# Attention on one Trainium2 core: exponentials of the first and third step transposed by the tensor engine instead of by DMA

## The chip, the cores and the metric

The kernel runs as one program on one core of a Trainium2 chip. The core has a tensor engine (PE, whose weight loads the profile lists as PEld), a vector engine (DVE), a scalar engine (ACT), GpSimd (POOL) and a sync engine (SP); 16 DMA engines move data for it. The metric is the device time of one execution in microseconds (us). Three executions of the kernel before took 1034.42, 1036.01 and 1037.72 us.

## What is computed

Three layers follow each other: causal attention with a cumulative bias, a mixture of eight experts with a greedy assignment of tokens, and a feed-forward layer. The change lies in the first one:

```python
# q, k, v: (4, 8, 576, 64), s: (4, 8, 576)
scores = scale * q @ k.T
cum = np.cumsum(np.maximum(s, 0.0), axis=-1)
bias = -(cum[:, :, :, None] - cum[:, :, None, :])
scores = np.where(causal, -1e9, scores + np.minimum(bias, 0.0))
attn = np.exp(scores - scores.max(-1, keepdims=True))
attn = attn / (attn.sum(-1, keepdims=True) + 1e-9)
out = attn @ v            # then x = out as (2304, 512)
# expert layer: logits = x @ w_gate; tokens taken in the order of all logits,
# 288 to an expert; relu(x[mask] @ w1[e]) @ w2[e]
# last layer: h = x @ w_in; (max(h,0) + alpha*min(h,0)) @ w_out
```

## The kernel before

The 32 heads are worked off as 16 pairs p, and each pair in four steps i: step 0 takes query blocks 0 and 1 of 128 rows (both heads), step 1 block 2, step 2 block 3, step 3 the last 64 queries of both heads. All operands are split into a high and a low half, and a product is made of three matmuls (high by high, low by high, high by low).

One step passes through these functions. `qk` (lines 166 to 191, PE) makes the scores in a PSUM tile `sc`, of which there are two, and adds the causal mask (line 181) and the bias (lines 182 and 191). The bias is a matmul of two small operands, SB and MB, which `load_bias` (lines 98 to 106) loads by DMA for two pairs at a time (`hb`, two pairs). `mins` (198, 199, DVE) takes the row minimum, `exps` (205, 208, ACT) writes the exponentials `e` in fp32, 128 queries by keys. For the product with v the keys must lie on the partitions. So `split_hi` (217, 221, 222, DVE) rounds e to fp16 in `eh`, `split_lo` (228, 231, 232, POOL) writes the remainder beside it, and `etr` (235, SP's queue) transposes both by one DMA from SBUF to SBUF into `et`. Four steps later (LAG=4) `av` (250 to 252 and 256 to 260, PE) multiplies et by v. `norm_main` (275, DVE), `finish` (286), and the logits of the router (`lg_T`, 294, four fp32 transposes by PE into a tile `tp`; `lg_act`, 298; `lg_pe`, 304; `lg_dve`, 309 and 310) close the pair. Of the PSUM tiles `tp` there are three.

Every engine works its instructions off in program order. That order is written by hand as a list of events: each function gets a time in steps, and a place within the step from the tuple ORDER, with a correction per function from the table SH:

```python
def at(t,eng,f,*a):
    u=t+ORDER.index(eng)/16+SH.get(key(f,a),0)
    ev.append((u,f,a))
```

From step 51 on, weights of the last layer are loaded early, and from step 54 on 11 of them are converted beside attention: three DVE instructions each (607 to 609), a copy on ACT (580) and a subtraction on POOL (581). After attention, `Router.phase` (line 489 on) and the expert and feed-forward layers run; their buffers are taken from pools that are opened when the pool `ap` of attention is closed, in the same memory (lines 947 to 950).

Of the kernel before, what the change touches and what calls it, by code (L numbers as in the profile page):

```python
# [28 lines left out]
LAG=4  # L29
LQ=(-12,-8)  # L30
LV=(-10,-9,-6,-5,-4)
LB=-7
V0=(1,1,1)
TI=-2
TQ=0;TD=1;TE='act2'
# [2 lines left out]
TP1=0  # L38

SH={"lg_pe": 1.83, "lt_act": 0.1, "v2_pool": 0.06, "spin": 0.17, "finish_tail": -0.2, "rd_4": 2.79, "lg_dve": 1.56, "load_bias": 0.68, "lt_pe": 1.31, "v3_act1": -0.94, "rd_2": -0.13, "v3_act0": 0.03, "etr2": 0.79, "rd_3": 1.2, "finish": 0.07, "lt_dve": 0.94, "av1": 1.9, "lt_T": -0.2, "av2": 0.43, "etr0": 0.23, "norm_main": 0.37, "v3_dve0": 1.63, "v3_dve1": 0.11, "av0": 1.59, "etr3": 0.23, "split_lo0": 0.07, "split_lo1": 0.6, "split_hi2": -0.23, "split_lo2": -0.13, "split_hi3": 0.63, "split_lo3": 0.77}  # L40
ORDER=('pe0','pe1','pe2','pe3','dve0','dveA','dveB','act1','sp','dve2','act2','dve3','pl','act3','ld')
def attention(tc, q, k, v, s, w_gate, xd, L, C, cp, ap, psum, dp, hook=None, rawp=None):
    rawp=rawp or ap
    nc=tc.nc
# [18 lines left out]
    nc.sync.dma_start(st, s.rearrange("b h s -> (b h) s"))  # L63
    for nm in 'qk': load_qk1(0,nm,0)

    SB=[ap.tile([128,2304],R,name=f'sb{i}') for i in range(2)]
    MB=[ap.tile([128,2,576],R,name=f'mb{i}') for i in range(2)]
    nc.vector.memset(SB[0].bitcast(F),0.0)
    mk=ap.tile([128,128],BF,name='mk'); nc.gpsimd.memset(mk,0.0)
    nc.gpsimd.affine_select(out=mk,in_=mk,pattern=[[-1,128]],compare_op=OP.is_ge,fill=1e9,base=0,channel_multiplier=1)  # L70
# [18 lines left out]
    def init_bias(i):  # L89
        sf=SB[i].bitcast(F); mf=MB[i].bitcast(F)  # L90
        nc.gpsimd.memset(mf,0.0)
        nc.gpsimd.memset(mf[64:66],1.0)
        if i: nc.vector.memset(sf,0.0)
        for h in range(4):
            r=32*(h%2)
            for c0,n in ((512*h,512),(2048+64*h,64)):
                nc.gpsimd.memset(sf[r:r+2,c0:c0+n],-1.0)
    def load_bias(hb):
        i=hb%2
        hv=chd[4*hb:4*hb+4]  # L100
        mf=MB[i].bitcast(F)
        mv=hv.rearrange("(p h) t s -> h t p s",h=2)
        for h in range(2): nc.sync.dma_start(mf[32*h:32*h+2], mv[h])
# [60 lines left out]
    PARTS={0:((0,0),(1,128)),1:((2,0),),2:((3,0),)}  # L164
    WID={0:384,1:384,2:512}
    def qk(p,i):
        hb=p//2; sb,mb=SB[hb%2],MB[hb%2][:,p%2]
        kh,kl=OPS['k',p]; qh,ql=OPS['q',p]
        sc=SM[p,i]=psum.tile([128,2,512],F,name='sc',bufs=2)
        if i<3:  # L170

            for ti,off in PARTS[i]:
                N=128*(ti+1)
                qs=slice(128*ti,128*ti+128)
                for n,(x,y) in enumerate(((qh,kh),(ql,kh),(qh,kl))):
                    for h in range(2):
                        r=slice(64*h,64*h+64)
                        nc.tensor.matmul(sc[:,h,off:off+N],x[r,qs],y[r,:N],start=(n==0),stop=False)  # L178
                for h in range(2):
                    c0=512*(2*(p%2)+h)+128*ti  # L180
                    nc.tensor.matmul(sc[:,h,off+N-128:off+N],idb,mk,start=False,stop=False,skip_group_check=True)
                    nc.tensor.matmul(sc[:,h,off:off+N],sb[:,c0:c0+128],mb[:,:N],start=False,stop=True)  # L182
        else:
            for h in range(2):
                o=sc[:,h,:288]
                ks=slice(288*h,288*h+288)
                nc.tensor.matmul(o,qh[:,512:640],kh[:,ks],start=True,stop=False)
# [723 lines left out]
def body(tc, q, k, v, s, w_gate, w1, w2, w_in, w_out, alpha, cfd, cbd, cid, out):  # L911
    nc = tc.nc
    with ExitStack() as c:
        cp = c.enter_context(tc.tile_pool(name="cp", bufs=1))
        dp = c.enter_context(tc.tile_pool(name="dp", bufs=1, space=bass.MemoryType.DRAM))
        c.enter_context(tc.manual_schedule())
        c.enter_context(nc.allow_low_precision(reason="integers and split operands"))
        cf = cp.tile([128, NCF], F, name="cf")
        ci = cp.tile([128, NCI], I, name="ci")
        cb = cp.tile([128, 256], BF, name="cb")  # L920
        nc.sync.dma_start(cf, cfd)
        L = cp.tile([128, 18, 8], F, name="L")
# [83 lines left out]
```

## Time and profile before

| | |
|---|---|
| median of three runs | 1036.01 us |
| the profiled execution | 1033.37 us, of which its span is 1031.6 us |
| busy in the span | PE 919.2, PEld 848.6, DVE 634.0, POOL 527.7, ACT 440.4 us |
| first row minimum of pair 0 (line 198) | starts at 15.83 us |
| last logits added (line 310) | start at 274.55 us |
| mean granted TensorE clock | 0.917 |

The views of the trace give times in us from the start of the span. PE's busy time counts each matmul to its modelled end, so a short gap can vanish in it. "Clock" is the share of full speed that TensorE was granted; in this trace it is 1.00 or 0.50 in nearly every stretch of 2 us, that is 2.4 or 1.2 GHz.

### The profile page before, as it was taken

How to read it: one execution, taken by the hardware profiler on the slowest of the kernel's cores; microseconds unless marked ns; L12 is line 12 of the kernel's file. 1: busy time of each engine (PE TensorE's matmuls, PEld its weight loads, DVE VectorE, ACT ScalarE, POOL GpSimd, SP SyncE). 2: the span in 40 equal slices, each digit the busy share in tenths (PEclk: the TensorE clock that was granted, in tenths of full speed). 3: DMA queues.
4: the chain of work that ended last, by engine and by line, in shares of the span. 5: the costliest groups of instructions: out<-in, count | busy, mean ns of one | idle time of the engine just before them, and what ended most of it. 6: DMA issues, size and time to landing. Idle time of an engine off the chain costs nothing.

```text
span 1031.6 us, 20621 instructions
## 1 busy us (share of the span) xinstructions
PE 919.2 (89%) x7883; PEld 848.6 (82%) x7883; DVE 634.0 (61%) x1238; ACT 440.4 (43%) x1106; POOL 527.7 (51%) x457
## 2 busy tenths in 40 slices
PE   6889998986427899899999999999999999999995
PEld 4667776765416789899999999999999899999994
DVE  6867667779894987776675645744654642442310
ACT  4656666544212334433334334334434344444432
POOL 6756766755423646744355346526625434634422
PEclk9968879867557999999999999999999999999997
DMA  5998999897577102222343315307304422522200
GB/s 167 206 215 170 213 193 204 198 265 141 146 265 233 40 20 79 81 65 87 63 111 104 51 46 147 73 8 162 89 9 90 123 52 61 152 53 65 52 1 24
DMA packets 219891, 116.59 MB, mean 113 GB/s; under 512 B 148304, under 2 KB 202960, under 8 KB 219792
## 3 DMA queue, kind: packets, MB, share of 16 engines
q1 hardware_dynamic: 180144, 96.78, 38.8%
q10 hardware_dynamic: 36576, 9.05, 5.8%
q0 software_dynamic: 3072, 9.44, 3.1%
q8 instruction: 62, 1.02, 0.4%
q14 instruction: 37, 0.30, 0.1%
HBM read 70.92 MB, written 9.58 MB: 78 GB/s over the span
## 4 chain that ended last, share of the span: by engine, by line
PE 55%; DVE 16%; DMA 10%; issue 8%; POOL 6%; ACT 3%; SPq 0%; POOLq 0%; DVEq 0%; ACTq 0%
PE hp L655 8%; PE hp L656 7%; PE hp L657 7%; PE acc L685 7%; PE acc L687 7%; PE acc L686 7%; DMA et<-eh 4%; DMA out_dram<-stg,idt 3%; PE sc L178 3%; PE sc L182 2%; PE mi L460 2%; DVE g L667 1%; DVE mn L198 1%; DVE eh L217 1%; DVE a L609 1%
## 5 line engine op out<-in xcount | busy, mean ns | idle before, releaser
L673 POOL TENSOR_TENSOR hh<-g,hh 128x288 fp32r<-128x288 f32 x128 | 118.4, 925 | 243.4 <-ACT hh L672 213.8
L667 DVE SCALAR_TENSOR_TENSOR g<-g,nal 128x288 f32<-128x288 f32 x128 | 79.6, 622 | 160.0 <-ACT g L666 153.3
L228 POOL TENSOR_TENSOR eh<-e,eh 128x768 f16<-128x768 f32 (+1 forms) x48 | 97.0, 2023 | 61.3 <-DVE eh L217 45.5
L581 POOL TENSOR_TENSOR w0r<-wraw,w0r 128x512 fp32r<-128x512 f32 x62 | 89.0, 1436 | 58.4 <-ACT w0r L580 58.2
L665 ACT ACTIVATE g<-hp 128x288 f32<-128x288 f32 x128 | 52.2, 408 | 131.5 <-PE hp L657 117.1
L672 ACT ACTIVATE hh<-g 128x288 fp32r<-128x288 f32 x128 | 56.9, 444 | 120.0 <-DVE g L667 117.9
L685 PE MATMUL acc<-hh,rB 128*128 128x288 f32 x352 | 106.1, 301 | 0.0
L687 PE MATMUL acc<-hh,rB 128*128 128x288 f32 x352 | 104.2, 296 | 0.0
L686 PE MATMUL acc<-hh,rB 128*128 128x288 f32 x352 | 104.0, 296 | 0.0
L205 ACT ACTIVATE e<-sc,mn 128x128 f32<-128x128 f32 (+3 forms) x128 | 66.0, 524 | 77.6 <-DVE mn L198 40.1
L655 PE MATMUL hp<-x2h,rB 128*128 128x288 f32 x320 | 90.8, 305 | 0.0
L656 PE MATMUL hp<-x2h,rB 128*128 128x288 f32 x320 | 89.7, 300 | 0.5 <-POOL rB L581 0.5
L661 DVE SCALAR_TENSOR_TENSOR hh<-hp,hh 128x288 fp32r<-128x288 f32 x64 | 29.0, 454 | 84.4 <-ACT hh L660 84.4
L686 PE MATMUL acc<-hh,w1r 128*128 128x288 f32 x256 | 76.7, 300 | 1.7 <-DVE w1r L581 0.8
L685 PE MATMUL acc<-hh,w1r 128*128 128x288 f32 x256 | 77.0, 301 | 0.0
L687 PE MATMUL acc<-hh,w1r 128*128 128x288 f32 x256 | 76.1, 297 | 0.0
L655 PE MATMUL hp<-xTh,w0r 128*128 128x288 f32 x256 | 73.7, 308 | 0.9 <-ACT xTh L708 0.6
L656 PE MATMUL hp<-xTh,w0r 128*128 128x288 f32 x256 | 73.0, 304 | 0.4 <-POOL w0r L581 0.4
L198 DVE TENSOR_REDUCE mn<-sc 128x2 f32<-128x256 f32 (+1 forms) x64 | 50.5, 810 | 33.5 <-PE sc L182 33.5
L685 PEld LDWEIGHTS acc<-hh,rB 128*128 128x128 f32 x352 | 66.4, 189 | 0.3
L687 PEld LDWEIGHTS acc<-hh,rB 128*128 128x128 f32 x352 | 66.5, 189 | 0.0
L581 POOL TENSOR_TENSOR w1r<-wraw,w1r 128x512 fp32r<-128x512 f32 x46 | 63.9, 1389 | 4.8 <-ACT w1r L580 4.6
(252 smaller groups left out, 2918.2 us busy)
## 6 DMA issues: line engine op xcount, KB each, us to landing
wraw<-in_moe_w_dram SPq DMA_DIRECT2D x128, 256.0 KB
rB<-in_moe_w_out_dram SPq DMA_DIRECT2D x11, 512.0 KB
qr<-in_q_dram SPq DMA_DIRECT2D x16, 320.0 KB
vr<-in_v_dram SPq DMA_DIRECT2D x40, 128.0 KB
rB<-in_moe_w_in_dram SPq DMA_DIRECT2D x10, 512.0 KB
kr<-in_k_dram SPq DMA_DIRECT2D x16, 288.0 KB
xd<-xm SPq DMA_DIRECT2D x16, 256.0 KB
rA<-in_moe_w_in_dram SPq DMA_DIRECT2D x4, 512.0 KB
```

The source lines that it names most:

```text
L198: nc.vector.tensor_reduce(mn[:,2*z:2*z+2],sc[:,:,off:off+128*(ti+1)],axis=AX.X,op=OP.min)
L205: nc.scalar.activation(e[:,h,off:off+N],sc[:,h,off:off+N],AF.Exp,bias=mn[:,2*z+h:2*z+h+1],scale=-1.0,accum_out=den[:,2*ti+h:2*ti+h+1])
L228: nc.gpsimd.tensor_sub(e4[:,:,1],e[:,:,:N],e4[:,:,0])
L581: lo_eng.tensor_sub(l,x,h.bitcast(F))
L655: nc.tensor.matmul(ps,wh[k],x[0][:,k],start=(k==0),stop=False)
L656: nc.tensor.matmul(ps,wl[k],x[0][:,k],start=False,stop=False)
L657: for k in range(4): nc.tensor.matmul(ps,wh[k],x[1][:,k],start=False,stop=(k==3))
L667: nc.vector.scalar_tensor_tensor(g,g2[:,1],self.nal[:,f:f+1],g,op0=OP.mult,op1=OP.add)
L673: nc.gpsimd.tensor_sub(hh[:,1],g,hh[:,0].bitcast(F))
L685: nc.tensor.matmul(a,wh[:,ds],hh[:,0],start=(f==0),stop=False)
L686: nc.tensor.matmul(a,wl[:,ds],hh[:,0],start=False,stop=False)
L687: nc.tensor.matmul(a,wh[:,ds],hh[:,1],start=False,stop=(f==last))
```

## The change

Steps 0 and 2 of every pair (PEI) no longer use split_hi, split_lo and the DMA. Instead, for each of the two heads, `etT` transposes e in fp32 blocks of 128 by 128 by PE into a tile tp (three blocks in step 0, four in step 2), `etA` (ACT) copies tp as fp16 into the high half of et, and `etL` (DVE) subtracts that from tp and writes the low half. Steps 1 and 3 keep the old way. The table ETS gives the places: for head 0, PE's place pe0 of the next step (before the scores), act2 and dve3; for head 1, pe3 and act3 of the next step, and dve1 of the one after it. ORDER gets the new place dve1, so the places behind it move by a sixteenth of a step.

The operands of the bias are held and loaded per pair, at half the size, 4 instead of 7 steps ahead (LB). The router's pool `rp` is opened before attention, with memory of its own.

```diff
-LB=-7
+LB=-4
...
-ORDER=('pe0','pe1','pe2','pe3','dve0','dveA',...,'act3','ld')
+ORDER=('pe0','pe1','pe2','pe3','dve0','dve1','dveA',...,'act3','ld')
+PEI=(0,2)
+ETS=(((1,'pe0'),(1,'act2'),(1,'dve3')),((1,'pe3'),(1,'act3'),(2,'dve1')))
...
-    SB=[ap.tile([128,2304],R,name=f'sb{i}') for i in range(2)]
-    MB=[ap.tile([128,2,576],R,name=f'mb{i}') for i in range(2)]
+    SB=[ap.tile([128,1152],R,name=f'sb{i}') for i in range(2)]
+    MB=[ap.tile([128,576],R,name=f'mb{i}') for i in range(2)]
...
-    def load_bias(hb):
+    def load_bias(p):
+        i=p%2
+        hv=chd[2*p:2*p+2]
+        for h in range(2): nc.sync.dma_start(MB[i].bitcast(F)[32*h:32*h+2], hv[h])
...
+    def etT(p,i,h):
+        if h==0: SM['T',p,i]=ap.tile([128,WID[i]//32,128],H,name=f'et{i}',bufs=2)
+        e=SM['e',p,i]
+        if h: SM.pop(('e',p,i)); SM.pop(('mn',p,i))
+        tp=SM['tp',p,i,h]=psum.tile([128,512],F,name='tp',bufs=TPB)
+        for j in range(WID[i]//128): nc.tensor.transpose(tp[:,128*j:128*j+128],e[:,h,128*j:128*j+128],idf)
+    def et2(p,i,h):
+        e4=SM['T',p,i].rearrange("p (h t j) q -> p h t (j q)",h=2,t=2)
+        return e4[:,h,0],e4[:,h,1],SM['tp',p,i,h][:,0:WID[i]]
+    def etA(p,i,h):
+        hi,lo,tp=et2(p,i,h)
+        nc.scalar.activation(hi,tp,AF.Copy)
+    def etL(p,i,h):
+        hi,lo,tp=et2(p,i,h); SM.pop(('tp',p,i,h))
+        nc.vector.tensor_sub(lo,tp,hi)
...
+    for p in range(1,NP): at(4*p+LB,'ld',load_bias,p)
...
-        at(t+1,'sp',split_hi,p,i); at(t+1,'sp',split_lo,p,i)
-        at(t+1+TD,TE,etr,p,i)
+        if i in PEI:
+            for h in range(2):
+                for (d,e),f in zip(ETS[h],(etT,etA,etL)): at(t+d,e,f,p,i,h)
+        else:
+            at(t+1,'sp',split_hi,p,i); at(t+1,'sp',split_lo,p,i)
+            at(t+1+TD,TE,etr,p,i)
...
+        rp = c.enter_context(tc.tile_pool(name="rp", bufs=1))
         with ExitStack() as a:
             ap = a.enter_context(tc.tile_pool(name="ap", bufs=1))
...
-            rp = a.enter_context(tc.tile_pool(name="rp", bufs=1))
```

PE, around the scores of a step 2 (`sc<-kh,qh 128x512`), before:

```order
L294 MATMUL tp<-cf,xm 128x128 x4
L178 MATMUL sc<-kh,qh 128x512 x2
L178 MATMUL sc<-kh,ql 128x512 x2
L178 MATMUL sc<-kl,qh 128x512 x2
L181 LDWEIGHTS idb
L181 MATMUL sc<-mk,idb 128x128
L182 MATMUL sc<-mb_92,sb_90 128x512
```

and now (L310 is the old L294, L243 is etT on the exponentials of step 0):

```order
L310 MATMUL tp<-cf,xm 128x128 x4
L243 MATMUL tp<-cf,e 128x128 x3
L178 MATMUL sc<-kh,qh 128x512 x2
L178 MATMUL sc<-kh,ql 128x512 x2
L178 MATMUL sc<-kl,qh 128x512 x2
L181 LDWEIGHTS idb
L181 MATMUL sc<-mk,idb 128x128
L182 MATMUL sc<-mb_95,sb_93 128x512
L181 LDWEIGHTS idb
L181 MATMUL sc<-mk,idb 128x128
L182 MATMUL sc<-mb_95,sb_93 128x512
L243 MATMUL tp<-cf,e 128x128 x3
```

Three transposes of head 0 now stand between the logits' transposes and the scores of step 2, and those of head 1 behind these scores, ahead of the next `av`; the eight of step 2 stand in the same way around the scores of the next pair's step 0.

DVE, from the row minimum of a step 1 (`L198 ... x1` ahead of L144 or L310) to the fp16 rounding of that step, before:

```order
L198 TENSOR_REDUCE mn<-sc 128x2
L144 TENSOR_SCALAR vh_e<-tp 128x1
L217 CAST eh<-e 128x2x384
L129 SCALAR_TENSOR_TENSOR ql<-qr,qh 128x640
L267 RECIPROCAL rd<-rd 128x9
L198 TENSOR_REDUCE mn<-sc 128x2
L217 CAST eh<-e 128x2x384
```

and now (L252 is etL; L326 is the old L310, L283 the old L267):

```order
L198 TENSOR_REDUCE mn<-sc 128x2
L326 TENSOR_TENSOR L<-L,tp 128x32
L144 TENSOR_SCALAR vh_e<-tp 128x1
L129 SCALAR_TENSOR_TENSOR ql<-qr,qh 128x640
L252 TENSOR_TENSOR et_2063<-tp,et_2063 128x384
L283 RECIPROCAL rd<-rd 128x9
L198 TENSOR_REDUCE mn<-sc 128x2
L252 TENSOR_TENSOR et_2063<-tp,et_2063 128x384
L217 CAST eh<-e 128x2x384
```

The first of the two CASTs is gone, and a subtraction from PSUM stands on either side of the row minimum of step 2.

SP, from one output of a pair (`xd<-xm`) to the next, before:

```order
L286 DMA xd<-xm 128x4x128
L235 DMA_TRANSPOSE et_1262<-eh 128x16x128
L289 DMA xd<-xtl 256x1x64 x2
L235 DMA_TRANSPOSE et_1300<-eh 128x9x128
L57 DMA kr<-in_k_dram 128x576
L235 DMA_TRANSPOSE et_1348<-eh 128x12x128
L61 DMA vr<-in_v_dram 128x256
L235 DMA_TRANSPOSE et_1417<-eh 128x12x128
```

and now:

```order
L302 DMA xd<-xm 128x4x128
L103 DMA mb_94<-chd 2x576 x2
L105 DMA sb_92<-chd 2x2x512
L106 DMA sb_92<-chd 2x2x64
L305 DMA xd<-xtl 256x1x64 x2
L235 DMA_TRANSPOSE et_1406<-eh 128x9x128
L60 DMA kr<-in_k_dram 128x576
L64 DMA vr<-in_v_dram 128x256
L235 DMA_TRANSPOSE et_1530<-eh 128x12x128
```

Two transposes of a pair are left of four, and the four small loads of the next pair's bias stand behind the output, now for every pair.

## Rows read from the trace of the kernel before

**Rows 1.** Stretches (us; busy, instructions; clock, DMA share, GB/s): pairs 0-12, 13-15, rest.
```profile
15.83:198.76 182.93, 163.47 (x1683) 128.84 (x1683) 130.53 (x220) 112.94 (x323) 121.34 (x90) 0.85 0.99 203
198.76:274.55 75.79, 55.34 (x516) 45.24 (x514) 68.81 (x97) 33.51 (x90) 46.28 (x32) 0.70 0.81 181
274.55:1031.60 757.05, 692.58 (x5637) 668.32 (x5637) 425.15 (x912) 290.59 (x688) 348.70 (x306) 0.95 0.33 85
```

**Rows 2.** Waits, 15.83 to 198.76 us: total, times, longest.
```profile
PE av L250 <- DMA et<-eh: 12.2, 7, 3.6
```

**Rows 3.** Stretches, same columns (PE PEld DVE ACT POOL): an idle PE, then ten us.
```profile
176.00:179.00 3.00, 0.00 (x0) 0.00 (x0) 1.49 (x3) 1.92 (x6) 1.55 (x1) 1.00 0.95 161
181.00:191.00 10.00, 10.00 (x58) 8.01 (x54) 4.37 (x10) 3.30 (x13) 4.16 (x4) 0.50 1.03 236
```

**Rows 4.** Stretches of one pair each, same columns: pairs 2, 7, 9 and 10.
```profile
39.80:51.73 11.93, 10.32 (x133) 8.02 (x131) 9.29 (x18) 8.85 (x25) 9.13 (x9) 1.00 1.09 206
113.33:126.00 12.67, 10.80 (x139) 8.60 (x137) 10.95 (x18) 8.56 (x25) 9.04 (x7) 1.00 1.11 220
140.70:155.95 15.25, 15.14 (x141) 11.96 (x140) 11.09 (x18) 8.82 (x26) 8.77 (x6) 0.69 1.03 192
155.95:168.68 12.73, 12.05 (x150) 9.85 (x148) 9.15 (x18) 8.74 (x25) 8.77 (x9) 1.00 1.04 205
```

**Rows 5.** DMA queues: packets, MB, share of 16 engines; q10 is ACT's.
```profile
q10 hardware_dynamic: 36576, 9.05, 5.8%
```

**Rows 6.** PE in order of time: start, us; at full and at half clock.
```profile
129.33 0.60 PE L294 MATMUL tp<-cf,xm 128*128 128x128 f32 x4
129.86 0.50 PE L178 MATMUL sc<-kh,qh 64*128 64x512 f32 x2
...
146.36 1.05 PE L294 MATMUL tp<-cf,xm 128*128 128x128 f32 x4
147.21 0.64 PE L314 MATMUL tp<-cf,xtl 128*128 128x128 f32 x2
```

**Rows 7.** Groups by shape, 0 to 262 us, and line 709: busy us, mean ns.
```profile
L217 DVE CAST eh<-e 128x768 f16<-128x768 f32 x32 | 21.6, 675 | 13.8 <-DMA et<-eh 11.6 <-ACT e L205 1.6 <-POOL kl L130 0.6
L217 DVE CAST eh<-e 128x1024 f16<-128x1024 f32 x16 | 18.3, 1143 | 5.2 <-DMA et<-eh 3.9 <-ACT e L205 0.8 <-issue 0.5
L228 POOL TENSOR_TENSOR eh<-e,eh 128x768 f16<-128x768 f32 x32 | 62.5, 1952 | 46.0 <-DVE eh L217 45.5 <-PE sc L182 0.5
L228 POOL TENSOR_TENSOR eh<-e,eh 128x1024 f16<-128x1024 f32 x16 | 34.7, 2166 | 15.3 <-DVE rd L269 15.3
L298 ACT ACTIVATE xT<-tp 128x512 f32<-128x512 f32 x15 | 8.9, 593 | 0.0
L709 DVE TENSOR_TENSOR xTl<-mi,xTh x6: 545/558/558, 315.5 to 421.7; 128x384 fp32r<-128x384 f32 x6
```

**Rows 8.** Lines 608 and 609, early conversions: ns minimum/median/maximum, first and last start.
```profile
L608 DVE SCALAR_TENSOR_TENSOR a<-rA,a x7: 691/1642/2019, 211.7 to 258.0; 128x512 int32<-128x512 int32 x7
L609 DVE SCALAR_TENSOR_TENSOR a<-rA,a x7: 1529/2009/2106, 215.6 to 259.7; 128x512 int32<-128x512 int32 x7
```

**Rows 9.** DVE and PE near the start, in order of time.
```profile
9.49 1.98 DVE L93 MEMSET sb<- 128x2304 f32 x1 [0.43 <-issue]
...
12.14 0.47 PE L178 MATMUL sc<-kl,qh 64*128 64x128 f32 x2 [2.55 <-DVE kl L130]
```

**Rows 10.** DVE from attention to the router, in order of time.
```profile
274.68 1.18 DVE L811 TENSOR_SCALAR nal<-al 128x16 f32<-128x16 f32 x1
...
275.86 0.30 DVE L496 TENSOR_REDUCE m<-L 128x18 f32<-128x144 f32 x1
```

**Rows 11.** Chain of waits near the start: start, us, what.
```profile
10.95 1.98 DMA sb<-chd
```

**Rows 12.** SP's queue and PE, from an output to the next pair's first bias.
```profile
127.92 0.38 SPq L286 DMA_DIRECT2D xd<-xm  x1
...
137.93 0.46 PE L182 MATMUL sc<-mb,sb 128*128 128x128 f32 x1
```

More of the change, by code (lines that the diff above doesn't have):

```diff
@@ L40 @@
 SH={"lg_pe": 1.83, "lt_act": 0.1, "v2_pool": 0.06, "spin": 0.17, "finish_tail": -0.2, "rd_4": 2.79, "lg_dve": 1.56, "load_bias": 0.68, "lt_pe": 1.31, "v3_act1": -0.94, "rd_2": -0.13, "v3_act0": 0.03, "etr2": 0.79, "rd_3": 1.2, "finish": 0.07, "lt_dve": 0.94, "av1": 1.9, "lt_T": -0.2, "av2": 0.43, "etr0": 0.23, "norm_main": 0.37, "v3_dve0": 1.63, "v3_dve1": 0.11, "av0": 1.59, "etr3": 0.23, "split_lo0": 0.07, "split_lo1": 0.6, "split_hi2": -0.23, "split_lo2": -0.13, "split_hi3": 0.63, "split_lo3": 0.77}
-ORDER=('pe0','pe1','pe2','pe3','dve0','dveA','dveB','act1','sp','dve2','act2','dve3','pl','act3','ld')
+ORDER=('pe0','pe1','pe2','pe3','dve0','dve1','dveA','dveB','act1','sp','dve2','act2','dve3','pl','act3','ld')
+PEI=(0,2)
+ETS=(((1,'pe0'),(1,'act2'),(1,'dve3')),((1,'pe3'),(1,'act3'),(2,'dve1')))
 def attention(tc, q, k, v, s, w_gate, xd, L, C, cp, ap, psum, dp, hook=None, rawp=None):
@@ L93, in init_bias @@
         if i: nc.vector.memset(sf,0.0)
[L94 to L97, printed above, removed]
-    def load_bias(hb):
[L99 to L103, printed above, removed]
+        for h in range(2):
+            for c0,n in ((512*h,512),(1024+64*h,64)):
+                nc.gpsimd.memset(sf[32*h:32*h+2,c0:c0+n],-1.0)
+    def load_bias(p):
+        i=p%2
+        hv=chd[2*p:2*p+2]
+        for h in range(2): nc.sync.dma_start(MB[i].bitcast(F)[32*h:32*h+2], hv[h])
         sv=hv.rearrange("h t s -> t h s")
-        nc.sync.dma_start(SB[i].bitcast(F)[64:66,0:2048].rearrange("t (h s) -> t h s",h=4), sv[:,:,0:512])
-        nc.sync.dma_start(SB[i].bitcast(F)[64:66,2048:2304].rearrange("t (h s) -> t h s",h=4), sv[:,:,512:576])
+        nc.sync.dma_start(SB[i].bitcast(F)[64:66,0:1024].rearrange("t (h s) -> t h s",h=2), sv[:,:,0:512])
+        nc.sync.dma_start(SB[i].bitcast(F)[64:66,1024:1152].rearrange("t (h s) -> t h s",h=2), sv[:,:,512:576])
     init_bias(0)
@@ L166, in qk @@
     def qk(p,i):
-        hb=p//2; sb,mb=SB[hb%2],MB[hb%2][:,p%2]
+        hb=p//2; sb,mb=SB[p%2],MB[p%2]
         kh,kl=OPS['k',p]; qh,ql=OPS['q',p]
@@ L179, in qk @@
                 for h in range(2):
-                    c0=512*(2*(p%2)+h)+128*ti
+                    c0=512*h+128*ti
                     nc.tensor.matmul(sc[:,h,off+N-128:off+N],idb,mk,start=False,stop=False,skip_group_check=True)
@@ L190, in qk @@
                 if h: nc.tensor.matmul(sc[:,h,224:288],idb,mkt,start=False,stop=False,skip_group_check=True)
-                nc.tensor.matmul(o,sb[:,2048+128*(p%2):2048+128*(p%2)+128],mb[:,ks],start=False,stop=True)
+                nc.tensor.matmul(o,sb[:,1024:1152],mb[:,ks],start=False,stop=True)
     def mins(p,i):
@@ L359, in attention @@
         for z in range(5): at(8*hb+LV[z],'ld',load_v1,hb,z)
-        at(8*hb+LB,'ld',load_bias,hb)
         v_events(hb,8*hb-1)
@@ L368, in attention @@
             if i<3 or h==1: at(t,'act1',exps,p,i,h)
-        at(t+1,'sp',split_hi,p,i); at(t+1,'sp',split_lo,p,i)
-        at(t+1+TD,TE,etr,p,i)
+        if i in PEI:
+            for h in range(2):
+                for (d,e),f in zip(ETS[h],(etT,etA,etL)): at(t+d,e,f,p,i,h)
+        else:
+            at(t+1,'sp',split_hi,p,i); at(t+1,'sp',split_lo,p,i)
+            at(t+1+TD,TE,etr,p,i)
         at(t+LAG,'pe2',av,p,i)
```

## The prediction

> **What bounds the kernel now.** I read the stretches first, cut at the row minima that begin the pairs. The stage after attention lasts 757 us [rows 1], and none of its instructions is changed. In the first 13 pairs (182.9 us, 14.07 us a pair) no engine is busy all the time: PE 163.5, DVE 130.5, POOL 121.3, ACT 112.9 us; but the 16 DMA engines have a share of 0.99 [rows 1]. So DMA sets the mean pace. How it does so is seen in the waits and then in short stretches. PE waits 12.2 us in 7 waits for a transposed tile et, at most 3.6 us [rows 2]; this is the direct loss. Behind such a gap comes a second one: from 176 to 179 us PE does nothing, and from 181 to 191 it runs at half clock (0.50, so 1.2 GHz), busy all the 10 us, with DVE, ACT and POOL under half busy [rows 3]. The mean clock of the 13 pairs is 0.85 [rows 1]; with two levels, that is 30% of the time at 1.2 GHz, 55 us. Pairs in which the clock stays at 1.00 last 11.93, 12.67 and 12.73 us, and PE is busy for 10.32, 10.80 and 12.05 us of them; pair 9, at 0.69, lasts 15.25 with PE busy for 15.14 [rows 4]. PE's work of a pair is thus about 11.06 us at full clock (the mean of the three). In pair 9 the low share is 9.5 us, so 5.75 us at full clock did 0.52 of the work and the 9.5 us the other 0.48: 19.8 us a pair at half clock.
>
> The last three pairs (75.8 us) are another stage: with the early conversions DVE is busy for 68.8 us [rows 1], and PE, at a mean of 0.70, for 55.3. DVE bounds them.
>
> **The change, part by part.**
>
> *DMA, SP, POOL.* A pair's transposes carry 1536, 1536, 2048 and 1152 columns of 128 fp16; the first and third go, 0.92 of 1.61 MB. The only DMA kind that I can price alone is the 39 transposes of ACT's queue, 9.05 MB in 5.8% of the span, 6.6 us of all 16 engines for 1 MB [rows 5]. By that 6.1 us a pair go, and DMA needs 13.9 - 6.1 = 7.9 us a pair. The per-pair bias adds 32 small issues for 32 transposes less. POOL loses one subtraction of 1.95 and one of 2.17 us a pair [rows 7], 4.1 of 9.3. What is left on both is hidden under PE.
>
> *PE.* It gains 6 + 8 = 14 fp32 transposes of 128x128 a pair. The same operation on xm takes from 129.33 to 129.86 for four at full clock, 0.133 us each, and 0.213 at half clock (146.36 to 147.21) [rows 6]. So 1.86 us a pair: 11.06 becomes 12.9 us at full clock, 19.8 becomes 22.8 at half.
>
> *ACT.* Two copies of 512 columns at 0.593 [rows 7] and two of 384, below that, are at most 2.4 us on top of 112.9/13 = 8.7: 11.1 us, under PE.
>
> *DVE.* A pair loses a CAST of 0.675 and one of 1.143, and gains two subtractions from PSUM of 384 columns (0.558 for the same shape in line 709) and two of 512 [rows 7]. No row has the latter; scaled by columns 0.74, with the 0.558 and twice it as ends. Sum +2.60 - 1.82 = +0.8 a pair: 10.0 becomes 10.8, again under PE's 12.9.
>
> *Pace of pairs 0 to 12.* What is late next when the transposed tiles are not? PE itself, the highest sum. An engine with work queued does not idle long, so I expect the clock to stay near 1.00. From 12.9 as lower end and 14.07 (nothing gained) as the other I take 13.2, near the lower end, because the full-clock pair with most work idles only 0.7 us beside its 12.05 [rows 4]. 13 x 13.2 = 171.6 against 182.9: **-11.3 us**.
>
> *Pairs 13 to 15.* DVE's 68.8 us grow by 3 x 0.8 = 2.4. Against that its early conversions run long beside POOL: line 608 takes 0.69 at the least but 1.64 at the median, line 609 has a median of 2.01 [rows 8]. Taking 0.69 as the free time for both, the 14 instructions of these two groups lose about 7 x 0.95 + 7 x 1.32 = 16 us. POOL works 46.3 us in this stage and loses 3 x 4.1 = 12.3 of them, 27%; if the loss shrinks alike, 4.3 us come back (ends: 0 and 16). DVE idles 7.0 us of the stage; a transpose waited for is half as likely, so I keep 3.0. 68.8 + 2.4 - 4.3 + 3.0 = 69.9 against 75.8: **-5.9 us**.
>
> *Start.* The clearing of SB, 1.98 us for 2304 columns, stands ahead of kl on DVE, for which PE then waits 2.55 us [rows 9]. At half the size 1.0 us goes: **-1.0 us**.
>
> *Edits at nothing.* The router's first reduction starts at 275.86, when DVE is done with line 811, which began behind the last logits [rows 10]; a buffer of its own starts no earlier. If that cover were gone it could be worth the 1.2 us of line 811 and no more. The bias load: a pair's four loads stand behind an output such as that at 127.92, and the next pair's first bias matmul comes at 137.93 [rows 12]. The first such load took 1.98 us [rows 11]. Even with the pair 1.5 us shorter it is there in time.
>
> The sum is -18.2 us. The profiled execution took 1033.4 us, 2.6 under the median of 1036.0, so I expect 1015.2 in an execution like it and **1017.8 us** in the median.
>
> **Rivals.**
>
> *The clock keeps falling (ends slower).* All PE waits need not come from DMA. If the low clock keeps its 30% of the time, a pair takes 1/(0.30/22.8 + 0.70/12.9) = 14.8 us, the 13 pairs gain 9.9 us, and with -6.9 from the rest the time is 1039. The point that decides is a pace of 14.6, a low share of about 0.28; at half of the old share (13.8 us) it would be 1025. For it: more PE work makes each slow stretch dearer. Against it: the slow stretch that I looked at follows a PE that does nothing at all [rows 3], while DMA was full. The Trainium skill, page "TensorE: Matmul & The Clock Gate", section "Part 4: PE-mode transpose", says that transposes don't count as work for the clock gate as matmuls do. By that rule the added 1.86 us a pair would not help to hold the clock, and this rival would be the forecast; no row here shows a long run of transposes, and the four at 129.33 ran at full clock among matmuls. Chance 0.13.
>
> *DVE's queue becomes the bound.* Each of the four subtractions of a pair waits for its copy on ACT, which stands behind exponentials, and two row minima of later steps stand behind a subtraction. With DVE at 10.8 us of work, a pace of 14.6 is reached when each of these waits is 0.95 us long; at 1.2 us the pace is 15.6, 13 pairs gain 19.9, and with the last three giving nothing it is 1055. For it: a copy of 0.59 and a handover make a part of such a wait plain. Against: DVE has 2.4 us free in 13.2. Chance 0.07.
>
> *The transposes that are left come late all the same.* If half of the bytes cost nearly as much DMA time as all, PE goes on waiting for step 1 and step 3 and nothing changes but the added work hides in the waits: 1035. Against: a share of 0.99 has to fall when bytes go. Chance 0.05.
>
> *More than forecast.* The busy time of PE counts modelled ends, so its real need may be 12.4; with DVE's contention gone by half (-8) and its idle time by 6: 13 x 12.4 gives -21.7, in all 1036 - 21.7 + 2.4 - 8 - 6 - 1 = 1002. Chance 0.10.
>
> **How the numbers follow.** Forecast 0.65, clock 0.13, DVE 0.07, no effect 0.05, more 0.10. The forecast's own bounds (pace 12.9 to 14.07, the last pairs from 0 to -12) reach from 1007 to 1035. With the bounds and the rivals near them, 1001 to 1038 holds about 8 in 10. 0.3%, 3.1 us, is about what a measurement of this kernel can tell from no change. Faster: 0.65 and 0.10, with a third of the clock's rival: 0.79. Within: the no-effect case and a third of the clock's: 0.09. Slower: the rest, 0.12.
>
> **What would show it.** In the changed profile: a DMA share near 0.6 to pair 12; a clock above 0.95 there; pairs near 13.2 us with PE busy for some 13; few waits of PE for et; POOL near 5.3 us a pair; lines 608 and 609 shorter. A clock still at 0.85, DVE idle in front of the new subtractions for more than 0.95 us each, or waits for et of the old size would prove the rivals. A share of DMA still near 1 would break the whole argument, and so would a stage after attention that is not 757 us long.

## The result, and the profile after

The changed kernel takes 1049.62 us (median of four runs, 1047.29 to 1050.30); the kernel before took 1035.40 beside it (1034.42 to 1037.72). The ratio is 1.013 with a 95% interval of 1.0106 to 1.0154. The forecast was 1017.8 us in a range up to 1038: it missed, on the slow side.

The parts that were forecast for DMA and POOL did happen. The page's busy times after, and the queue that carries the transposes:

```profile
PE 938.2 (89%) x8107; PEld 865.8 (83%) x8107; DVE 626.9 (60%) x1270; ACT 470.1 (45%) x1170; POOL 449.9 (43%) x417
...
q1 hardware_dynamic: 121840, 82.10, 30.0%
```

POOL works 450 us instead of 528. The same three stretches as in [rows 1] (pairs 0 to 12, pairs 13 to 15, the rest; columns as there):

```profile
14.30:212.24 197.94, 175.15 (x1851) 139.19 (x1852) 133.80 (x245) 135.02 (x373) 63.35 (x64) 0.91 0.58 131
212.24:290.17 77.93, 59.73 (x573) 48.74 (x570) 63.42 (x103) 39.77 (x104) 30.03 (x25) 0.75 0.51 131
290.17:1048.50 758.33, 695.56 (x5637) 671.70 (x5637) 422.03 (x912) 291.89 (x689) 349.59 (x306) 0.95 0.33 84
```

DMA's share falls from 0.99 to 0.58, and yet the first 13 pairs take 15.0 us longer. The profiled span grew by 16.9 us: the start gives 1.5 back, pairs 0 to 12 cost 15.0, pairs 13 to 15 cost 2.1, and the rest 1.3. So the cause lies in the pairs. PE's waits there, total, times, longest (before, [rows 2], it was et from DMA):

```profile
PE tp L320 <- DVE et L252: 7.1, 5, 1.4
PE tp L243 <- DVE L L325: 4.8, 3, 1.6
PE tp L243 <- ACT e L205: 4.4, 8, 1.3
PE tp L330 <- DVE L L326: 3.2, 2, 1.6
```

No wait for et is left in these pairs. PE now waits to write a tile `tp`. L320 is lg_pe, L243 etT, L330 lt_T, L252 etL, L325 and L326 lg_dve (from av to lt_dve, line numbers are 16 higher than before). Pairs 3 to 6 one by one, to be held against [rows 4]:

```profile
52.60:66.40 13.80, 11.96 (x144) 9.76 (x142) 11.35 (x22) 11.13 (x30) 4.50 (x4) 1.00 0.58 137
66.40:83.68 17.28, 15.49 (x154) 11.97 (x152) 9.84 (x20) 9.87 (x28) 5.38 (x6) 0.80 0.51 115
83.68:98.08 14.40, 12.79 (x157) 10.53 (x155) 11.35 (x21) 11.28 (x31) 4.49 (x4) 1.00 0.63 141
98.08:117.38 19.30, 17.51 (x161) 13.80 (x159) 9.72 (x22) 9.97 (x28) 5.38 (x6) 0.73 0.59 100
```

Two things are to be seen. From pair 2 on, pairs at full clock last about 14 us, not the 13.2 of the forecast. And from pair 4 on every even pair falls to half clock for a part of its time. Pair 6 in order of time shows what stands ahead of that fall:

```profile
98.76 0.38 PE L139 MATMUL tp<-vs,onesf 128*128 128x1 f32 x2
99.01 0.63 PE L243 MATMUL tp<-cf,e 128*128 128x128 f32 x4
99.68 0.60 ACT L249 ACTIVATE et<-tp 128x512 f16<-128x512 f32 x1 [2.89 <-PE tp L243]
100.31 0.69 DVE L252 TENSOR_TENSOR et<-tp,et 128x512 f16<-128x512 f32 x1 [1.22 <-ACT et L249]
101.05 1.33 PE L320 MATMUL tp<-wgs,xT 128*128 128x8 f32 x8 [1.41 <-DVE et L252]
...
102.38 0.31 ACT L299 ACTIVATE xtl<-tp,rd 64x64 f32<-64x64 f32 x1
...
105.86 0.15 DVE L144 TENSOR_SCALAR vh_e<-tp 128x1 int32<-128x1 int32 x1
```

There are three tiles tp. One holds the sum of squares of v (L139, v2_pe, one column) from 98.76 until DVE reads it at 105.86 (L144, v2_dve): 7.1 us. The second holds the product of step 3 with v (av's last part), until L299 reads it at 102.38. So lg_pe can only have the third, and that one has just been filled by the transposes of L243: it must go through ACT's copy and DVE's subtraction first. PE stands still for 1.41 us. These two stretches show that it was at full clock before, and that from 101.6 us on, while the logits still ran, it was at half clock:

```profile
98.50:100.90 2.40, 1.14 (x11) 0.73 (x7) 1.18 (x2) 1.22 (x5) 0.00 (x0) 1.00 1.20 131
101.60:111.20 9.60, 9.22 (x43) 6.52 (x43) 2.94 (x8) 4.08 (x12) 3.67 (x5) 0.50 0.49 133
```

The other wait, 1.6 us in the odd pairs, has another maker. DVE around the logits of pair 5's stretch, before (L160 is v3_dve, L310 lg_dve, L198 the row minimum of step 1):

```profile
85.70 0.87 DVE L160 SCALAR_TENSOR_TENSOR vhl<-vr,vcc,vhl 128x640 f16<-128x640 f32 x1
86.50 0.17 DVE L310 TENSOR_TENSOR L<-L,tp 128x32 f32<-128x32 f32 x1
87.08 0.96 DVE L198 TENSOR_REDUCE mn<-sc 128x2 f32<-128x768 f32 x1 [0.41 <-PE sc L182]
```

and after:

```profile
87.39 0.96 DVE L198 TENSOR_REDUCE mn<-sc 128x2 f32<-128x768 f32 x1 [0.39 <-PE sc L182]
88.26 0.88 DVE L160 SCALAR_TENSOR_TENSOR vhl<-vr,vcc,vhl 128x640 f16<-128x640 f32 x1
89.06 0.17 DVE L326 TENSOR_TENSOR L<-L,tp 128x32 f32<-128x32 f32 x1
...
89.38 0.41 PE L330 MATMUL tp<-cf,xtl 128*128 128x128 f32 x2 [1.59 <-DVE L L326]
```

The minimum has passed ahead of two instructions. Counted from a pair's first step, its lg_dve stood at 13.2475 in the table, and the minimum of step 1 three pairs on at 13.25; the new name dve1 in ORDER moves lg_dve by a sixteenth, to 13.31. It frees its PSUM tile later by one minimum.

### The profile page after: what moved, and what is told of

It reads as the page before. It is cut to its first block, busy times and chain, and to the rows that moved or that the text cites. A ratio compares the mean times of both kernels' runs of the same rounds, so it can differ in the third digit from the quotient of the medians.

```text
span 1048.5 us, 21051 instructions
## 1 busy us (share of the span) xinstructions
PE 938.2 (89%) x8107; PEld 865.8 (83%) x8107; DVE 626.9 (60%) x1270; ACT 470.1 (45%) x1170; POOL 449.9 (43%) x417
## 4 chain that ended last, share of the span: by engine, by line
PE 59%; DVE 18%; issue 7%; ACT 6%; DMA 4%; POOL 3%; SPq 1%; POOLq 0%; DVEq 0%; ACTq 0%
PE hp L675 8%; PE acc L705 8%; PE hp L676 8%; PE hp L677 8%; PE acc L707 7%; PE acc L706 7%; PE sc L178 2%; DVE a L628 2%; ACT e L205 2%; PE tp L243 2%; PE sc L182 2%; PE mi L480 2%; DVE mn L198 1%; DMA out_dram<-stg,idt 1%; DVE et L252 1%
## 5 line engine op out<-in xcount | busy, mean ns | idle before, releaser
L687 DVE SCALAR_TENSOR_TENSOR g<-g,nal 128x288 f32<-128x288 f32 x128 | 76.6, 598 | 161.9 <-ACT g L686 151.8
L198 DVE TENSOR_REDUCE mn<-sc 128x2 f32<-128x256 f32 (+1 forms) x64 | 50.5, 810 | 30.5 <-PE sc L182 30.5
L252 DVE TENSOR_TENSOR et<-tp,et 128x384 f16<-128x384 f32 (+1 forms) x64 | 39.8, 622 | 47.1 <-ACT et L249 47.1
```

Of the source, the lines that this page charges most:

```text
L198: nc.vector.tensor_reduce(mn[:,2*z:2*z+2],sc[:,:,off:off+128*(ti+1)],axis=AX.X,op=OP.min)
L687: nc.vector.scalar_tensor_tensor(g,g2[:,1],self.nal[:,f:f+1],g,op0=OP.mult,op1=OP.add)
```

## The experiments

Theory A: the loss comes from the three tiles tp, which now have more users and are held too long by others. Rivals: B, the other edits; C, the in-order queues of DVE and ACT; D, transposes do not hold the clock. Each ratio is against runs of the kernel before on the same chip, and stands with its 95% interval; the quotient of the two medians can differ from it by a quarter of a per cent.

**First run: all steps by the DMA again** (the edits beside the transposes stay).

```diff
-PEI=(0,2)
+PEI=()
```

> All four steps' exponentials go by the DMA again; what stays of the change is the bias operands per pair, the router's buffers apart, and the extra name in the order list. Theory A (the loss comes with the transposes, through the shared PSUM buffers tp): the time is the kernel before's within 0.3%, 1032 to 1038 us, pairs 0 to 12 near 183 us. Rival B (the loss comes from what was moved beside the transposes: more bias loads in SyncE's queue, places shifted in the order, other addresses): at least half of the loss stays, 1042 us or more.

1047.46 us, ratio 1.0111 (1.0076 to 1.0147). Theory A, as it was put, falls here, and rival B holds: 1.1% is lost without one transpose more on PE.

**Second to fourth run: the two holders of tp read earlier on DVE,** each alone and both.

```diff
-"lg_dve": 1.56
+"lg_dve": 0.65        # second and fourth run
...
-SH={"lg_pe": 1.83,
+SH={"v2_dve": -1.08, "lg_pe": 1.83,        # third and fourth run
```

> The changed kernel with lg_dve placed right behind lg_pe on VectorE (0.91 of a step earlier), so that lg_pe's PSUM buffer comes free before the next transposes ask for one. Theory A: the 1.6 us wait of the transposes for lg_dve goes in pairs 3, 5, 7, 9, 11 (and 13): about 5 x 1.6 = 8 us less, 1041 us; the 1.4 us wait of lg_pe in pairs 4, 6, 8, 10, 12 and the half clock behind it stay. Rival C (VectorE's and ScalarE's in-order queues set the pace, the PSUM wait is only where it shows): another wait of like length comes up on TensorE, 1047 to 1052 us.

> The changed kernel with v2_dve placed right behind v2_pe on VectorE (1.08 steps earlier), so that v2's PSUM buffer, held for about 7 us, is free when lg_pe asks for one. Theory A: the 1.41 us wait of lg_pe goes in pairs 4, 6, 8, 10, 12, and with it the half clock behind each; these pairs fall from 17.8 to about 14.2 us: 5 x 3.6 = 18 us less, 1032 us. Rival D (transposes do not hold the clock, wait or no wait): the waits go but the half clock stays, about 5 x 1.4 = 7 us less, 1043 us. Rival C: 1047 to 1052 us.

> The changed kernel with both places moved (lg_dve and v2_dve). Theory A: the gains add, 8 + 18 = 26 us less: 1024 us, granted clock near 1.00 to pair 12, pairs 0 to 12 in about 172 us. Rival D: 1049.6 - 15 = 1035 us with the half clock still in every second pair. Rival C: 1047 to 1052 us with other waits in the place of these.

Second: 1057.56 us, 1.0218 (1.0178 to 1.0257). The waits for lg_dve went, but PE waits 10.7 us for the exponentials instead, and DVE itself 6.3 us for lg_pe: rival C, and worse than it said. Third: 1031.27 us, 0.9969 (0.9939 to 1.0000), as theory A said. In the third run's pair 6, v2_dve follows v2_pe at once and lg_pe waits for nothing:

```profile
101.29 0.38 PE L139 MATMUL tp<-vs,onesf 128*128 128x1 f32 x2
101.71 0.16 DVE L144 TENSOR_SCALAR vh_e<-tp 128x1 int32<-128x1 int32 x1
102.00 0.42 PE L320 MATMUL tp<-wgs,xT 128*128 128x8 f32 x3
```

Its pairs 4 and 6:

```profile
72.45:86.77 14.32, 13.25 (x164) 10.99 (x161) 9.88 (x20) 9.85 (x28) 5.47 (x6) 1.00 0.63 123
100.60:114.81 14.21, 13.41 (x169) 11.29 (x167) 10.02 (x22) 9.85 (x28) 5.47 (x6) 1.00 0.74 136
```

Pairs 4, 6, 8, 10 and 12 together last 71.3 us instead of 89.0: 17.7 us less, 18 were expected. 7.1 of them are the waits. The other 10.6 I put down to the half clock: in the changed kernel these pairs had mean clocks of 0.73 to 0.90, which makes about 34 us at 1.2 GHz, and here all five have 1.00. So rival D falls for these pairs, with as many transposes. It is not the whole of the third run's profile, though. Pair 3 lasts 19.1 us there at a clock of 0.64, instead of 13.8 at 1.00, and pairs 0 to 12 together are only 11.5 us shorter (186.4 against 197.9). The fourth run, 1038.23 us, 1.0020 (0.9984 to 1.0056), is no better than the third. Its profile has half clock for 13 us or more from 65 and from 181 us, soon after waits of 1.9 us for exponentials, with no wait of lg_pe. The gains don't add, and from pair 2 on the pairs at full clock last 13.8 to 14.4 us with either wait or without. Something else holds them there.

**Fifth to eighth run: the shift of the places.** Theory E says that the first run's loss is the shift alone. In the fifth the kernel before gets nothing but the name; the others take the shift back (`dve1` gets the place 4.5 between dve0 and the next) in the first run's kernel, in the changed one, and in the changed one with v2_dve early.

```diff
-ORDER=(...,'dve0','dveA',...)
+ORDER=(...,'dve0','dve1','dveA',...)        # fifth run, on the kernel before
...
-    u=t+ORDER.index(eng)/16+SH.get(key(f,a),0)
+    u=t+(4.5 if eng=='dve1' else ORDER.index(eng))/16+SH.get(key(f,a),0)   # sixth to eighth
```

> The kernel before with one edit: the new name dve1 put into the order list, used by nothing. All places behind dve0 come 1/16 of a step later, and on VectorE the row minimum of step 1 passes ahead of v3_dve and lg_dve in every pair. Theory E (this shift is the loss: lg_dve and v2_dve then keep their PSUM buffers through one minimum longer, and TensorE's next transposes wait for them): about the first run's 1.011, 1042 to 1048 us at before 1033. Rival F (the loss of the first run is the bias loads per pair, or the router's buffers): no change, ratio 0.997 to 1.003.

> All four steps by the DMA with bias per pair and the router's buffers apart, and the places not shifted: the first run with the shift alone taken back. Theory E: ratio 0.995 to 1.003. Rival F: 1.008 to 1.014 as in the first run.

> The changed kernel with the shift alone taken back: the new name has a place of its own between dve0 and the next, so that lg_dve and v3_dve stand ahead of step 1's minimum again. Theory E: the 1.6 us waits for lg_dve go from pairs 3, 5, 7, 9, 11; the 1.41 us waits of lg_pe behind v2 and the half clock after them stay: about 8 us less than the changed kernel, ratio near 1.005. Theory E with the whole of the first run's 1.1% in it: ratio 1.002 or below. Rival C (in-order queues: another wait takes the place): ratio 1.010 or more.

> The shift taken back and v2_dve placed right behind v2_pe. Theory A with E: both waits gone, pairs near 14 us or below at full clock to pair 12: ratio 0.985 to 0.992, better than the third run's 0.997. Rival C: no better than the third run, 0.995 to 1.002.

Fifth: 1048.80 us, 1.0112 (1.0078 to 1.0146). Sixth: 1038.45, 1.0028 (1.0004 to 1.0051). Theory E holds for the kernel that uses DMA: v3_dve and lg_dve behind one minimum a pair (beside it only a few loads late in SP's queue change places) cost it 1.1%, and the bias and the router's buffers together 0.3% (0.0 to 0.5). How the swap does it is shown only in part. These are PE's two largest waits of pairs 0 to 12 in the fifth run (L294 is lg_T; L144 is v2_dve, which stands right behind lg_dve):

```profile
PE sc L178 <- ACT e L205: 10.0, 8, 2.9
PE tp L294 <- DVE vh_e L144: 6.2, 5, 1.2
```

The clock is 0.74 in these pairs, against 0.85 before, and 0.59 to 0.62 in pairs 4, 6, 8, 10 and 12; why the exponentials come late there no run isolates.

But the seventh, 1048.49 us, 1.0133 (1.0112 to 1.0155), is no better than the changed kernel. There the shift costs nothing that the medians show (the profiled execution is the fastest of the four, and its pairs 0 to 12 are 5.5 us shorter than the changed kernel's). The waits of lg_pe stay (7 times, 10.9 us, up to 262 us). The 1.6 us waits for lg_dve go, but in pairs 3, 7 and 11 waits of 1.58 us for exponentials stand in their place, and those for exponentials come to 8.7 us in pairs 0 to 12 instead of 4.4: rival C. The eighth, 1032.85 us, 0.9989 (0.9968 to 1.0010), equals the third: rival C. Its clock is 1.00 from pair 4 to pair 13, and pairs 5 to 12 still take 14.14 us on the mean, the even ones 13.3 and the odd ones 15.0. PE's largest wait is for exponentials, 14.7 us in 12 waits in pairs 0 to 12, 1.5 us each in pairs 3, 4, 7, 8, 11 and 12 (not in every pair, as the expectation of the ninth run has it). Followed back from that wait in pair 7:

```profile
117.79 0.49 PE L182 MATMUL sc<-mb,sb 128*128 128x512 f32 x1
...
118.38 0.68 ACT L125 ACTIVATE kh<-kr 128x576 fp32r<-128x576 f32 x1
118.95 0.59 ACT L314 ACTIVATE xT<-tp 128x512 f32<-128x512 f32 x1
119.43 0.50 ACT L249 ACTIVATE et<-tp 128x384 f16<-128x384 f32 x1
119.96 0.56 DVE L252 TENSOR_TENSOR et<-tp,et 128x384 f16<-128x384 f32 x1 [1.54 <-ACT et L249]
120.55 1.17 DVE L198 TENSOR_REDUCE mn<-sc 128x2 f32<-128x1024 f32 x1
...
121.83 0.69 ACT L205 ACTIVATE e<-sc,mn 128x512 f32<-128x512 f32 x1 [0.28 <-DVE mn L198]
...
122.67 0.55 PE L243 MATMUL tp<-cf,e 128*128 128x128 f32 x3 [1.56 <-ACT e L205]
```

The scores of step 2 are done at 118.28. Their minimum starts 2.3 us later, because it stands on DVE behind the subtraction of step 0's head 0; that one waits for its copy, and the copy stands on ACT behind kh, for which POOL waits, and xT, which lg_pe reads at 127.46.

**Ninth to twelfth run: that chain, and two controls.**

```diff
-ETS=(((1,'pe0'),(1,'act2'),(1,'dve3')),
+ETS=(((1,'pe0'),(1,'sp'),(1,'dve3')),        # ninth, on the eighth: etA ahead of kh and xT
...
-    ... at(t+d,e,f,p,i,h)
+    ... at(*((t+2,'dve1') if f is etL and i==0 else (t+d,e)),f,p,i,h)   # tenth, on the ninth
...
-PEI=(0,2)
+PEI=(0,)                                     # eleventh, on the eighth
...
-SH={"lg_pe": 1.83,
+SH={"v2_dve": -1.08, "lg_pe": 1.83,          # twelfth, on the kernel before
```

> The eighth kernel (no shift, v2_dve early) with the copy of head 0 (etA) put ahead of T_act of k and lg_act on ScalarE: the eighth's trace has VectorE idle for 1.54 us until that copy, with the minimum of step 2 standing behind the subtraction, and TensorE's transposes of step 2 then wait 1.5 us for the exponentials in every pair. Theory G (this chain, copy - subtraction - minimum - exponentials - transposes, sets the 14.1 us a pair at full clock): the wait falls by about 1 us a pair, 13 us in all, ratio 0.986 to 0.990. Rival H (TensorE's own 12.8 us and the waits that come next set it): ratio 0.996 to 1.002.

> The ninth kernel with the subtraction of step 0, head 0, also put behind the minimum of step 2 on VectorE, so that this minimum waits for no copy at all. Theory G: another 0.5 to 1 us a pair less than the ninth, ratio 0.977 to 0.986. Rival A again (the subtraction now frees its PSUM buffer a step's minimum later, and TensorE's next transposes wait for that): no better than the ninth, waits for the subtraction L252 of some 1 us in every pair.

> The eighth kernel with step 0 alone on TensorE and step 2 by the DMA again. TensorE has 8 transposes a pair less, VectorE a wide cast for two subtractions, and the DMA's share goes up to about 0.8. Theory G and A: fewer users of the PSUM buffers, no wait of step 2's transposes for its exponentials: pairs near 13 us, ratio 0.985 to 0.992. Rival I (the DMA transposes come late again and the clock falls behind the waits for et, as in the kernel before): ratio 0.998 to 1.004.

> The kernel before with v2_dve placed right behind v2_pe, nothing else. Control for the third and eighth runs. Theory A (v2's place costs only where transposes ask for the buffers): ratio 0.997 to 1.003. Rival J (the gain of the early v2_dve has nothing to do with the transposes): ratio 0.985 to 0.990, as much as it gave the changed kernel.

Ninth: 1020.90 us (four runs, 1020.37 to 1022.26) against 1033.50, 0.9865 (0.9826 to 0.9905). It beats both kernels, and the time is what theory G said. Its three stretches:

```profile
14.27:187.14 172.87, 160.28 (x1860) 131.20 (x1860) 136.75 (x246) 134.69 (x373) 69.94 (x64) 0.99 0.66 150
187.14:260.18 73.04, 54.96 (x563) 45.11 (x560) 62.65 (x103) 39.63 (x104) 32.01 (x25) 0.81 0.58 141
260.18:1019.10 758.92, 695.34 (x5637) 670.42 (x5637) 423.10 (x912) 291.37 (x689) 350.76 (x306) 0.95 0.32 84
```

172.87 us for 13 pairs are 13.3 a pair, at a clock of 0.99. The copy now stands before kh and xT. In pair 8 the subtraction waited 2.33 us for it in the eighth run, and PE 1.51 us for exponentials behind that; in the ninth the subtraction waits 1.27 us, and PE's wait is gone. The eighth run's row first:

```profile
133.96 0.56 DVE L252 TENSOR_TENSOR et<-tp,et 128x384 f16<-128x384 f32 x1 [2.33 <-ACT et L249]
```

```profile
125.71 0.49 ACT L249 ACTIVATE et<-tp 128x384 f16<-128x384 f32 x1
126.23 0.56 DVE L252 TENSOR_TENSOR et<-tp,et 128x384 f16<-128x384 f32 x1 [1.27 <-ACT et L249]
```

The gain of 10.1 us over the eighth run (182.94 to 172.87) isn't spread as expected. 5.0 us lie in the even pairs from 4 to 12, which go from 13.3 to 12.3 us. 4.6 lie in pairs 0 to 3: in the eighth run a wait of 1.93 us for exponentials in pair 2 came with half clock from 49 to 56 us, and in the ninth that wait is 0.87 us and no such stretch follows. The odd pairs from 5 to 11 gain 0.5 us together. In pair 7 the wait for the copy falls from 1.54 to 0.48 us, and the pair lasts 15.07 us, as before (15.01). What holds the odd pairs near 15 us no run here isolates.

Tenth: 1021.38 us, 0.9865 (0.9826 to 0.9904), no gain over the ninth, so the rest of that chain no longer sets the pace; the waits for L252 that rival A expected did not come either. Eleventh: 1034.07 us, 0.9992 (0.9962 to 1.0023). With three steps by DMA its share is 0.85 in pairs 0 to 12 and the clock 0.87. The ratio is rival I's, its mechanism only in part: PE's waits for et are 3.8 us in these pairs (12.9 before), and the two longest stretches at half clock, from 49 and from 80 us, 13 us or more each, begin at waits of 1.6 us for the minimum of step 3. Twelfth: 1037.19 us, 1.0021 (0.9995 to 1.0047). The early v2_dve is worth nothing where no transposes ask for the tiles.

**Thirteenth and fourteenth run: which of the edits are needed,** on the changed kernel with the shift left in: etA early alone, and with v2_dve early.

```diff
-ETS=(((1,'pe0'),(1,'act2'),(1,'dve3')),
+ETS=(((1,'pe0'),(1,'sp'),(1,'dve3')),        # both
...
-SH={"lg_pe": 1.83,
+SH={"v2_dve": -1.08, "lg_pe": 1.83,          # fourteenth
```

> The changed kernel with etA of head 0 ahead of T_act of k and lg_act on ScalarE, v2_dve left late and the shift kept. If the two causes add: the 1.41 us waits of lg_pe and the half clock behind them stay in pairs 4, 6, 8, 10, 12, but the wait for the exponentials is shorter: 8 to 13 us less than the changed kernel, ratio 1.000 to 1.006. If the v2 wait is the only bound as long as it is there: no gain, 1.010 to 1.015.

> The changed kernel with both places moved (v2_dve early, etA of head 0 first) and the shift kept: the smallest edit that should restore the forecast. If the shift does not matter: the ninth run's 0.9865 within 0.003, pairs 0 to 12 near 173 us. If it does, because lg_dve keeps its buffer through a minimum: 1.6 us waits for it in every second pair, ratio 0.990 to 0.996.

Thirteenth: 1047.99 us, 1.0155 (1.0105 to 1.0205): no gain in the medians, though pairs 0 to 12 of its profile are 4.3 us shorter; the five waits of lg_pe are there as before, and the clock is 0.80 to 0.90 in all five pairs. Fourteenth: 1026.57 us, 0.9931 (0.9908 to 0.9954), with waits of 1.6 us for lg_dve in the odd pairs (here from 14 to 200 us) and of 0.8 us in even ones:

```profile
PE tp L243 <- DVE L L325: 4.8, 3, 1.6
PE tp L330 <- DVE L L326: 4.8, 3, 1.6
```

So the shift, which cost nothing in the changed kernel's medians, costs about half a per cent once the two other waits are gone: 0.66 by the two ratios, which come from two chips, 0.5 by the medians, and 3.3 us between the two profiled executions, 3.1 of them in pairs 0 to 12. With v2_dve early the shift also moves v2_dve behind the minimum of step 0, so these are not lg_dve's and v3_dve's alone. The three delays hide each other (etA early with the shift back and v2_dve late was not run):

| kernel | ratio to before |
|---|---|
| changed | 1.0130 |
| shift back (7th) / etA early (13th) | 1.0133 / 1.0155 |
| v2_dve early (3rd) | 0.9969 |
| v2_dve early, shift back (8th) | 0.9989 |
| v2_dve early, etA early (14th) | 0.9931 |
| all three (9th) | 0.9865 |

## Why the prediction was wrong

By its own steps, in us against the profiled span of before; the ninth run is the changed kernel with three places moved and the same work:

| step | forecast | changed | ninth run |
|---|---|---|---|
| start | -1.0 | -1.5 | -1.6 |
| pairs 0 to 12 | -11.3 | +15.0 | -10.1 |
| pairs 13 to 15 | -5.9 | +2.1 | -2.8 |
| the rest | 0 | +1.3 | +1.9 |
| sum | -18.2 | +16.9 | -12.5 |

**The engines' work was right.** Forecast and measured in the ninth run, us a pair over pairs 0 to 12: PE 12.9 and 12.3 (160.28/13), ACT 11.1 and 10.4, DVE 10.8 and 10.5, POOL 5.3 and 5.4, DMA's share near 0.6 and 0.66. The subtraction of 512 columns, guessed at 0.74, takes 0.69. "13.2 us a pair" is what this work can do; the ninth run does 13.3. That it comes so near is in part luck: from pair 4 on the even pairs take 12.3 us and the odd ones 14.9. The trace of before had such an odd pair at full clock, pair 5, which the prediction's three left out (columns as in [rows 4]):

```profile
83.77:98.51 14.74, 12.60 (x155) 9.85 (x152) 10.94 (x19) 8.83 (x26) 9.93 (x7) 1.00 1.02 196
```

**The step that failed** is "What is late next when the transposed tiles are not? PE itself, the highest sum." The costs of ACT and DVE were put at nothing, "under PE", by sums of busy time. A sum doesn't see in which order an engine takes its work, nor how long a buffer is held. The text ahead of the prediction has the three tiles tp in it, and the prediction counts fourteen more transposes without counting who holds what they write to: four more users a pair, each through ACT and DVE, beside v2's tile that lies for 7.1 us. By the third run that is 17.7 us in five pairs. The chain by way of etA then holds the pairs near 14.1 us on the mean: by the step from the eighth run to the ninth (182.94 to 172.87 us for pairs 0 to 12) another 10.1, of which PE's waits for exponentials make 7.1 (14.7 us down to 7.6).

**"I expect the clock to stay near 1.00"** failed with it. The rival of the clock came true in part. Its pace was passed (15.2 us a pair against 14.6), but the mean clock is 0.91 and not the 0.85 that was to be its sign, and the low share is 18% and not the 28% that were to decide: the rest is waiting at full clock. And its place was another: not a clock that falls anywhere, but five pairs, behind one wait. The Trainium skill, page "TensorE: Matmul & The Clock Gate", section "Part 4: PE-mode transpose", says that transposes don't count as PE work for the clock in the way matmuls do. As a reason against the change that isn't borne out: the ninth run keeps 0.99 with fourteen more transposes a pair. What the rows do show in agreement with it is weaker: in pair 6 four transposes, the wait and eight small matmuls of the logits stand between 99.01 and 102.38, and the clock fell at 101.6. In the last section two stretches with the same transposes and the same wait differ in their clock.

**The rival on DVE's queue** named the right chain ("waits for its copy on ACT, which stands behind exponentials, and two row minima of later steps stand behind a subtraction") and got a chance of 0.07. DVE's longest wait in pairs 0 to 12 of the changed kernel (total, times, longest) is just this:

```profile
DVE et L252 <- ACT et L249: 38.9, 36, 2.4
```

That is 1.08 us for each of the 36 that waited, but there are 52, four a pair: 3.0 us a pair, under the 3.8 (four times 0.95) that were to decide. DVE's work of 10.3 us a pair and these waits make 13.3, not 15.2, so DVE isn't the bound by its sum either. It is the place of the waits that costs, ahead of a minimum on which PE depends, as the ninth run showed in the even pairs. That its weight was judged by "2.4 us free in 13.2" repeats the failed step: free time elsewhere in the pair doesn't help an instruction that stands behind a wait.

**Edits at nothing.** The bias and the router's buffers cost 0.3% (sixth run). The shift of the places was described but not followed to the minimum of step 1. It costs 1.1% on the kernel before, nothing that shows in the changed kernel's medians, and about half a per cent in the repaired one.

**Pairs 13 to 15.** DVE's early conversions got shorter, but not both: line 628 (608 before, [rows 8]) keeps its median, 629 (609) falls from 2.01 to 0.68 us:

```profile
L628 DVE SCALAR_TENSOR_TENSOR a<-rA,a x7: 693/1647/2020, 223.6 to 273.6; 128x512 int32<-128x512 int32 x7
...
L629 DVE SCALAR_TENSOR_TENSOR a<-rA,a x7: 629/681/1525, 229.0 to 275.3; 128x512 int32<-128x512 int32 x7
```

By the medians that alone is 9.3 us less (7 x 1.33), where 4.3 were forecast. DVE works 63.4 us instead of the 66.9 expected. But it isn't the bound any more: it idles for 14.5 of the 77.9 us, not for 3. 8.1 of them are seven waits of the subtractions for their copies, and 4.0 are waits for scores, while PE runs at 0.75 and lg_pe's wait comes here too, three times, 2.1, 1.7 and 3.0 us long. In the ninth run DVE still idles 10.4 us. The term failed by its idle time, in which the copies were put at nothing.

## What to carry to other kernels

When work moves from one engine to others, count for each buffer it writes who else holds one, from when to when, before any sum of busy times; a tile that waits 7 us for a read of 0.15 us takes a third of a ring of three. Where an engine works in order, look for what stands behind an instruction that waits for another engine, and put that wait behind the next thing the bottleneck needs. In a table of hand-made places, a new name is a change of all the places behind it: compare the two orders for swaps. And when a repair brings nothing, it may be hidden by another delay: only the three together came near the gain that was forecast (1020.9 us, 1017.8 forecast).

## What was not expected of the hardware

In the changed kernel the clock fell to 0.50 behind each of the five waits of 1.41 us ahead of lg_pe (pairs 4 to 12), and in the seventh run behind four of five. These stretches were 3.5 to 10.5 us long. Yet it stayed at 1.00 in pairs 3, 5, 7, 9 and 11 of the changed kernel with a wait of 1.6 us, the longer gap, ahead of etT or lt_T. One could think that the work around the gap decides: ahead of lg_pe's wait PE had done v2's matmul and four transposes, and behind it came the logits; ahead of the other stood transposes too, and behind it transposes and then scores. The fourteenth run speaks against that. Its pairs 7 and 11 have the same wait of 1.60 us for lg_dve, ahead of the same three transposes and the same scores, at 111.33 and at 168.35 us. In pair 7 the clock was at 0.50 from 113.5 to 116 us; in pair 11 it stayed at 1.00:

```profile
105.75:121.07 15.32, 13.72 (x151) 11.45 (x149) 10.93 (x22) 10.99 (x30) 4.48 (x4) 0.89 0.63 143
162.77:176.95 14.18, 12.58 (x158) 10.46 (x156) 11.58 (x21) 10.99 (x30) 4.48 (x4) 1.00 0.63 135
```

So neither the length of a gap nor the instructions next to it tell these two apart, and what makes the difference stays open. That the fall goes from pairs 4, 6, 8, 10 and 12 when lg_pe's wait goes is shown by the third run, in one profile.
